# The ending of a top-32 attention with highway layer: the verdict flag through a ones matmul and ScalarE, hints ahead of the skip branch, and spare matmuls

## Chip, cores and metric

One core of a Trainium2 chip runs the whole program. The metric is the device time in microseconds (us) of one launch; the median of several launches is quoted. The five engines are TensorE (PE in the profile, with PEld for its weight loads), VectorE (DVE), ScalarE (ACT), GpSimd (POOL) and SyncE (SP), which mostly issues DMAs. Each has an instruction stream of its own and waits for the others through semaphores.

## What is computed

The inputs are `q`, `k`, `v` of shape 8 x 8 x 576 x 64 (batch, heads, rows, head width) and a highway layer on the 4608 x 512 matrix of all heads side by side.

```python
scores = scale * np.matmul(q, k.transpose(0, 1, 3, 2))
kth = np.partition(scores, -top_k, axis=-1)[..., -top_k:-top_k + 1]   # top_k = 32
scores = np.where(scores >= kth, scores, -1000000000.0)
attn = np.exp(scores - np.max(scores, axis=-1, keepdims=True))
attn = attn / (np.sum(attn, axis=-1, keepdims=True) + 1e-09)
x = heads_side_by_side(np.matmul(attn, v))
H = np.maximum(x @ w_h, 0.0)
T = 1.0 / (1.0 + np.exp(-(x @ w_t + b_t)))
out = (T * H + (1.0 - T) * x).astype(np.float32)
```

## The kernel before, in words

Query rows are taken in groups of 128 of one batch; a group holds eight heads, and two heads (a "pair", `n`) are worked on at a time: 144 pairs in 144 steps (lines 1006 to 1099), about 5.6 us each. In step `n`, PE makes the scores of pair `n+1` (`scores`, line 220), ACT copies them into a buffer `z` (`evac`, line 242), DVE folds and searches the scores of earlier pairs for the 32nd largest value (`tree`, `folds`, `tops`, `rest`, with POOL computing the minima of the folds), ACT makes a penalty `pen` from the threshold (`mask`), PE transposes score plus penalty (`trans`, `parts`), ACT takes the exponential into `et`, and PE multiplies with the values (`av`) five steps after the scores. The highway layer of a finished group (`ffn_x`, `ffn_h`, `ffn_t`, `ffn_d`, `ffn_e`, `ffn_o`) is spread over later steps.

The class `PinnedCore` (line 41) keeps every instruction of the five engines in the order in which the source issues it, except what is issued through plain `nc.sync`. All pinned instructions are therefore shown with line L36; they are told apart by their tiles. Each engine takes its instructions strictly in order, so an instruction that waits holds up all behind it.

After the loop comes a hand-written ending (lines 1101 to 1167) for the last three pairs, `m` = 141 to 143, the group before the last (`gp`) and the last group (`gl`):

- `ffn_x`, `ffn_h`, `ffn_t` of `gp` run on PE; `final_norm(gl, i0, i1)` (line 592) divides a stretch of columns of the last group by its sums: DVE writes `scales` and then `x`.
- `final_turn(gl, i0, i1, bank)` (line 607) lets PE transpose these columns into `xtps`, and DVE (or ACT, for one middle stretch) scale them into `xT`. It is done for the columns 0 to 2, then 2 to 3, then 3 to 4 (in units of 128). `final_h` and `final_t` multiply `xT` with the two weight matrices on PE.
- `ffn_d(gp)`, `ffn_e(gp)`, `ffn_o(gp)` are DVE's last work on `gp` (tiles `xh`, `d`, `d`, `o`; 512 columns each), and SP sends `o` away (line 791).
- `judge_lists`, `judge_scales`, `judge_last` (lines 980 to 993) reduce checks over the whole run to one number per partition, `bad`: whether the fast search of the 32nd value may have been wrong for any row.
- `final_o` (line 655) makes the last group's output in two halves on DVE: `d`, `o`, then SP sends the first half away, then `d`, `o`, then ACT sends the second. Only then `judge` (line 995) turns `bad` into one integer: PE transposes it into a row (`bps`), DVE takes the maximum (`flag_f`) and casts it (`flag`).

Every engine then loads `flag` into a register (line 1169) and branches (line 1170): if it is above 0, a general path (lines 1171 to 1212) computes everything anew, in a loop over batches; otherwise all engines jump over it to the end of the program, where SP waits for every DMA queue and all engines meet. With these inputs the general path is skipped. The general path is long: the jump passes some 1,340 instructions on PE, 520 on DVE, 170 on ACT, 150 on SP and 50 on POOL.

`WARM` (line 23) and `spin` (line 949) already put matmuls of no use into the opening: `spin(n)` multiplies the zero tile `idle` with itself `n` times into a PSUM tile of the pool `ztps`.

Of the kernel before, what the change touches and what calls it, by code (L numbers as in the profile page):

```python
# [9 lines left out]
ALU = mybir.AluOpType  # L10
AX = mybir.AxisListType
FP32 = mybir.dt.float32
# [7 lines left out]
J = 4  # L20
NZ = 3
NPEN = 3
WARM = {1: 9, 2: 7, 3: 8}


# [43 lines left out]
class Ops:  # L69
# [582 lines left out]
            if i1 == n_g:  # L652
                nc.scalar.activation(tp, tp, AF.Tanh)

    def final_o(self, g, dsts, queues, finish):


        vec, P = self.nc.vector, self.P
        W = self.dm // 2
        n = P // len(dsts)  # L660
        o = self.fpool.tile([P, self.dm], FP32, tag="o", name="o")
        for j, tp in enumerate(g.tp):
            cs = slice(j * W, (j + 1) * W)
            vec.scalar_tensor_tensor(
                out=g.d[:, cs], in0=tp, scalar=1.0, in1=g.d[:, cs],
                op0=ALU.add, op1=ALU.mult,
            )
            vec.tensor_tensor(o[:, cs], g.d[:, cs], g.x[:, cs], ALU.subtract)
            for i, dst in enumerate(dsts):
                queues[j].dma_start(dst[:, cs], o[i * n : (i + 1) * n, cs])  # L670
        finish()

    def ffn_bank(self, g, name, other=False):
        if g.last:
# [120 lines left out]
def kernel(  # L795
# [10 lines left out]
    nc = tc.nc  # L806
    P = nc.NUM_PARTITIONS
# [13 lines left out]
    def const(shape, dt, name):  # L821
        return consts.tile(shape, dt, tag=name, name=name)
# [20 lines left out]
    for i in range(2):  # L843
        vt = const([P, H, nck, DE], BF16, f"v{i}")
        nc.gpsimd.memset(vt[:], -1.0)
        vbufs.append(vt)
    cst = const([P, P], BF16, "cst")
    nc.gpsimd.memset(cst[:], 0.5 / float(P))
    room = const([P, NG, H, 4], FP32, "room")
# [15 lines left out]
    with ExitStack() as cm:  # L865
# [18 lines left out]
        def out_rows(g):  # L884
            if not g.rem:
                r0 = g.b * S + g.qt
                return [out[r0 : r0 + JP : J, :]]
            ends = [(g.b + i) * S for i in (0, 1)]
            return [out[r1 - R : r1, :] for r1 in ends]
# [56 lines left out]
        ops.load_first(pr, queue, 2, H)  # L946
        ops.load_rest(pr, "krest", queue, 2, H)
        ops.load(pr, "kin", 2, queue)
        def spin(n):
            if n:  # L950
                warm = ops.ztps.tile([P, 512], FP32, tag="zt", name="warm")
            for _ in range(n):
                ops.nc.tensor.matmul(
                    warm[:], idle[:, 0:P], idle[:], start=True, stop=True
                )
# [17 lines left out]
        step = 0  # L973
        ok = const([P, 4], FP32, "ok")
        bad = const([P, 5], FP32, "bad")
        flag_f = const([1, 1], FP32, "flag_f")
        flag = const([1, 1], I32, "flag")
        vec = ops.nc.vector

# [14 lines left out]

        def judge():
            bps = ops.zrps.tile([P, 512], FP32, tag="zr", name="bps")
            ops.nc.tensor.transpose(bps[0:1, 0:P], bad[:, 4:5], ident[:])
            vec.tensor_reduce(flag_f[:], bps[0:1, 0:P], op=ALU.max, axis=AX.X)
            vec.tensor_copy(flag[:], flag_f[:])

        late, fill, opening = [], [], []
        def values(m):
            g, pi = pairs[m]
            ops.av(m, g, pi, preps[g.b]["vb"])

        while step <= NPR:
            n = step
            if have(n):
                ops.tree(n)
                if n < 2:  # L1010
                    ops.minima(n, ops.folds(n, *pairs[n], []))
                    opening += ops.lists(n, *pairs[n])
                    ops.run(opening, 1)
                elif n % 2:
                    nq = n // 2 + 1
                    ops.minima(nq, ops.folds(nq, *pairs[n - 1], fill))
                    fill = []
                if NHP <= n + 1 < 2 * NHP:
                    ops.turn(pr, "qin", n + 1 - NHP, None, 1)
                if n == NHP:  # L1020
                    ops.load(pr, "qin", 3, None, None, 1)
                if n == 2 * NHP:
                    ops.turn_rest(pr, 0, NHP, ("qrest",))
            if n == 5:
                load_weights()
            if have(n - 4):
                ops.mask(n - 4, *pairs[n - 4], tis=(0,))
            kind = fg = None
            nextg = None
            if ffn and (ffn[0][0] != "x" or n % 2):  # L1030
                kind, fg = ffn.pop(0)
                if kind == "t" and ffn and ffn[0][0] == "x":
                    nextg = ffn.pop(0)[1]
            if have(n - 5):
                values(n - 5)
            if have(n - 4):
                ops.mask(n - 4, *pairs[n - 4], tis=(1,))
            if have(n + 1):
                g, pi = pairs[n + 1]
                ops.scores(n + 1, g, pi, preps[g.b])  # L1040
                ops.evac(n + 1)
                if n + 2 < NHP:
                    ops.turn(pr, "kin", n + 2, True)
            spin(WARM.get(n, 0))
            if kind == "x":
                ops.ffn_x(fg)
            if kind == "h":
                ops.ffn_h(fg)
                ops.ffn_r(fg)
                ops.ffn_d(fg)  # L1050
            if nextg:
                ops.ffn_x(nextg)
            if kind == "t":
                ops.ffn_t(fg)
                if n < NPR - 1:
                    ops.ffn_e(fg)
                    ops.ffn_o(fg, *out_rows(fg))
            if n == 3:
                ops.values_rest(pr)
                ops.values(pr, 0)  # L1060
            if n == 4:
                ops.values(pr, 1)
            ended = False
            if have(n - 5):
                g, pi = pairs[n - 5]
                ended = pi == len(g.pairs) - 1 and (not g.rem or g.r0 > 0)
            if n % 2:
                gens = ops.lists_rest(n // 2 - 1, *pairs[n - 3]) if have(n - 3) else []
                late = gens[2:]
                gens = gens[0:2]  # L1070
                ops.run(gens)
                ops.run(late, 2)
            else:
                ops.run(late)
                if n == 2:
                    gens = opening
                else:
                    gens = ops.lists(n - 2, *pairs[n - 2]) if have(n - 2) else []
                ops.run(gens, 2 * (n > 2))
                if ended:  # L1080
                    ops.norm(pairs[n - 5][0])
                ops.run(gens, 3)
                if have(n + 1):
                    gens, fill = gens[0:2], gens[2:4]
                ops.run(gens)
            if have(n - 4):
                ops.trans(n - 4)
            if ended and not pairs[n - 5][0].last:
                ops.norm_heads(pairs[n - 5][0])
            for piece in pieces.pop(n, []):  # L1090
                piece()
            if n % 2 == 0 and have(n - 3):
                g, pi = pairs[n - 3]
                if pi == len(g.pairs) - 1:
                    ops.settle(g)
            if ended:
                g = pairs[n - 5][0]
                ffn += [("x", g), ("h", g), ("t", g)]
            step += 1
# [12 lines left out]
        ops.ffn_o(groups[-3], *out_rows(groups[-3]))  # L1112
        ops.mask(m, *pairs[m])
        values(m - 1)
        ops.trans(m)
        ops.ffn_x(gp)
        values(m)
        late = ops.lists_rest(m // 2 + 1, *pairs[m + 1])
        gens, late = late[0:2], late[2:]
        ops.run(gens)  # L1120
# [7 lines left out]
        ops.final_norm(gl, 0, 2)  # L1128
        ops.trans(m + 1)
        ops.ffn_r(gp)  # L1130
        ops.ffn_d(gp, h)
        judge_lists()
        judge_scales()
        part, ends = ops.parts(
            m + 2,
            banks[3],
            (banks[0], ops.fps.tile([P, 512], FP32, tag="fp", name="zt")),
        )
        ends()
        part(0)  # L1140
        part(1)
        values(m + 1)
        ops.final_turn(
            gl, 0, 2, ops.ztps.tile([P, 512], FP32, tag="zt", name="xtps")
        )
        ops.ffn_tanh(gp)
        gl.ps = ops.fps.tile([P, 512], FP32, tag="fp", name="hps")
        ops.final_norm(gl, 2, 3)
        ops.ffn_e(gp)
        values(m + 2)  # L1150
        ops.final_h(gl, 0, 2)
        ops.final_turn(
            gl, 2, 3, ops.ztps.tile([P, 512], FP32, tag="zt", name="xtps")
        )
        ops.final_norm(gl, 3, 4)
        ops.ffn_o(gp, *out_rows(gp))
        ops.final_t(gl, 0, 2)
        ops.final_turn(
            gl, 3, 4, ops.ztps.tile([P, 512], FP32, tag="zt", name="xtps")
        )  # L1160
        ops.final_h(gl, 2, 3)
        ops.final_t(gl, 2, 3)
        judge_last(gl)
        ops.final_h(gl, 3, 4)
        ops.ffn_d(gl)
        ops.final_t(gl, 3, 4)
        ops.final_o(gl, out_rows(gl), (nc.sync, ops.nc.scalar), judge)

    taken = nc.values_load(flag[0:1, 0:1], min_val=0, max_val=1)
    with tc.If(taken > 0):  # L1170
        with tc.For_i(0, B, 1) as b:
            with ExitStack() as cm:
                ops = Ops(cm, tc, shared, exact=True)
# [69 lines left out]
```

## Time and profile before

| what | value |
|---|---|
| median of 4 runs | 834.43 us (833.31, 834.35, 834.52, 834.64) |
| profiled execution, its own time | 833.48 us |
| its span, first to last instruction | 831.7 us |
| DVE busy | 814.8 us, 98% of the span |
| ACT, POOL, PE busy | 91%, 85%, 85% |
| mean granted clock of PE | 0.985 |
| chain that ended last, by engine | DVE 91%, PE 3%, ACT 2%, POOL 2%, issue 1% |
| last busy instruction (DVE's cast into `flag`) | 824.67 to 824.81 us |

How to read it: the profiled execution lasted 1.78 us longer than its span, which lies around the first and the last instruction. The profile counts as busy only what an engine itself computes; register loads, branches, semaphore waits and DMA issues are done by an engine's sequencer and have a "q" after the engine's name (DVEq). The chain of waits goes back from the last busy instruction, so what comes after 824.8 us has to be read from the instructions of the lines 1169, 1170 and 1238 (the program's end).

### The profile page before, as it was taken

How to read it: one execution, taken by the hardware profiler on the slowest of the kernel's cores; microseconds unless marked ns; L12 is line 12 of the kernel's file. 1: busy time of each engine (PE TensorE's matmuls, PEld its weight loads, DVE VectorE, ACT ScalarE, POOL GpSimd, SP SyncE). 2: the span in 40 equal slices, each digit the busy share in tenths (PEclk: the TensorE clock that was granted, in tenths of full speed). 3: DMA queues.
4: the chain of work that ended last, by engine and by line, in shares of the span. 5: the costliest groups of instructions: out<-in, count | busy, mean ns of one | idle time of the engine just before them, and what ended most of it. 6: DMA issues, size and time to landing. Idle time of an engine off the chain costs nothing.

```text
span 831.7 us, 20149 instructions
## 1 busy us (share of the span) xinstructions
PE 703.1 (85%) x6586; PEld 486.6 (59%) x6586; DVE 814.8 (98%) x4176; ACT 760.9 (91%) x1522; POOL 708.8 (85%) x457
## 2 busy tenths in 40 slices
PE   8788888888898888788888898878988888888874
PEld 4565566565666555565566565656556665555553
DVE  5999999999999999999999999999999999999996
ACT  4899999899999999899999999989999999988984
POOL 5888888789889888888889988888888989887991
PEclk9999999999999999999999999999999999999998
DMA  7564334234153432333325242323413211111221
GB/s 182 137 107 84 65 90 77 60 71 93 29 109 77 77 90 38 73 65 72 83 52 101 63 113 39 65 58 65 115 39 67 50 27 39 40 39 27 40 39 43
DMA packets 105184, 58.12 MB, mean 70 GB/s; under 512 B 82288, under 2 KB 91888, under 8 KB 105072
## 3 DMA queue, kind: packets, MB, share of 16 engines
q1 hardware_dynamic: 93200, 37.47, 17.3%
q0 software_dynamic: 11056, 19.01, 15.9%
q8 instruction: 53, 0.87, 0.4%
q14 instruction: 59, 0.48, 0.2%
q10 hardware_dynamic: 816, 0.30, 0.1%
HBM read 30.67 MB, written 18.35 MB: 59 GB/s over the span
## 4 chain that ended last, share of the span: by engine, by line
DVE 91%; PE 3%; ACT 2%; POOL 2%; issue 1%; DMA 0%; DVEq 0%; POOLq 0%
DVE w L36 51%; DVE m L36 19%; DVE hi L36 11%; DVE hh L36 6%; DVE h L36 3%; PE ps L36 1%; POOL hh L36 1%; POOL hi L36 1%; ACT z L36 1%; PE warm L36 1%; ACT x L36 0%; DVE scales L36 0%; DMA out_dram<-t 0%; ACT pen L36 0%; POOL t L36 0%
## 5 line engine op out<-in xcount | busy, mean ns | idle before, releaser
L36 PE MATMUL ps<-kq 64*128 64x64 f32 (+3 forms) x1280 | 203.6, 441 | 48.6 <-DVE hi L36 42.2
L36 ACT ACTIVATE pen<-z,m 128x576 bf16<-128x576 f32 x286 | 225.7, 790 | 1.7 <-DVE m L36 1.5
L36 PE MATMUL zt<-ident,z 128*128 128x128 f32 x1140 | 213.2, 280 | 2.3 <-ACT xT L36 2.3
L36 PE MATMUL zt<-nident,pen 128*128 128x128 bf16 x1148 | 205.7, 220 | 0.0
L36 ACT ACTIVATE z<-ps 128x1152 f32<-128x1152 f32 x143 | 161.7, 1131 | 42.7 <-PE ps L36 38.9
L36 POOL TENSOR_TENSOR hi<-z,hi 128x1152 int32<-128x1152 int32 (+1 forms) x72 | 188.2, 2614 | 11.1 <-DVE hh L36 5.5
L36 POOL TENSOR_TENSOR hi<-hi,z 128x1152 int32<-128x1152 int32 (+1 forms) x72 | 189.2, 2628 | 5.6
L36 PEld LDWEIGHTS ps<-kq 64*128 64x128 f32 (+1 forms) x1280 | 103.4, 177 | 143.1 <-issue 80.7
L36 PEld LDWEIGHTS zt<-ident,z 128*128 128x128 f32 x1140 | 161.5, 142 | 17.1 <-ACT xT L36 3.2
L36 ACT ACTIVATE et<-zt 128x512 bf16<-128x512 f32 x287 | 162.0, 601 | 6.0 <-PE zt L36 2.2
L36 POOL TENSOR_TENSOR hh<-hi,hh 128x576 int32<-128x576 int32 x71 | 104.2, 1467 | 71.1 <-DVE w L36 71.0
L36 PEld LDWEIGHTS <-pen 128*128 128x128 bf16 x1440 | 152.3, 106 | 16.2 <-ACT pen L36 10.9
L36 DVE MAX8 m<-w 128x8 f32<-128x168 f32 x576 | 159.0, 315 | 0.0
L36 PE MATMUL zr<-v,et 128*128 128x65 bf16 (+1 forms) x1590 | 98.5, 196 | 48.5 <-ACT et L36 41.4
L36 PEld LDWEIGHTS <-et 128*128 128x128 bf16 (+1 forms) x1600 | 68.8, 101 | 87.6 <-ACT et L36 85.5
L36 DVE MAX8 w<-hi 128x8 f32<-128x288 f32 x288 | 115.7, 441 | 0.0
L36 DVE TENSOR_TENSOR hi<-ps,z 128x576 f32<-128x576 f32 x142 | 104.5, 736 | 0.9 <-ACT z L36 0.9
L36 POOL TENSOR_TENSOR hh<-hh,hi 128x576 int32<-128x576 int32 x71 | 100.3, 1412 | 5.6
L36 DVE MAX8 w<-hh 128x8 f32<-128x72 f32 x576 | 96.7, 218 | 0.0
L36 DVE MATCH_REPLACE8 w<-m,w 128x168 f32<-128x168 f32 x288 | 88.6, 313 | 0.0
L36 PE MATMUL zr<-ident,z 128*128 128x128 f32 x284 | 67.9, 293 | 8.7 <-ACT xs L36 8.7
L36 ACT ACTIVATE x<-xs,scales 128x64 f32<-128x64 f32 x272 | 68.2, 336 | 0.0
(104 smaller groups left out, 1168.8 us busy)
## 6 DMA issues: line engine op xcount, KB each, us to landing
x<-d POOLq DMA_DIRECT2D x34, 256.0 KB, 3.9
vin<-in_v_dram SPq DMA_DIRECT2D x8, 1024.0 KB, 5.4
kin<-in_k_dram SPq DMA_DIRECT2D x63, 128.0 KB, 3.3
out_dram<-d SPq DMA_DIRECT2D x30, 256.0 KB, 2.3
out_dram<-t POOLq DMA_DIRECT2D x30, 256.0 KB, 4.1
qin<-in_q_dram SPq DMA_DIRECT2D x56, 128.0 KB, 2.9
qrest<-in_q_dram SPq DMA_DIRECT2D x8, 128.0 KB, 3.2
vrest<-in_v_dram SPq DMA_DIRECT2D x8, 128.0 KB, 3.1
```

The source lines that it names most:

```text
L36: return self._tc.keep_in_program_order(fn(*args, **kw))
```

## The change

The verdict is moved off DVE and ahead of `final_o`: `bad` is multiplied with a column of ones (a new constant, set by POOL at the start), which gives the sum over partitions in one number, and ACT copies it into the integer `flag`. The two DVE instructions `flag_f` and `flag` go. In program order, ACT makes this copy ahead of its DMA of the second half, and SP loads the flag before it issues the DMA of the first half.

Ahead of `final_h(gl, 3, 4)` every engine gets one hint instruction that says that its branch at line 1170 will be taken, that is, that the general path will be jumped over.

The ending is reordered: `final_turn(gl, 0, 2)` is moved from behind `values(m + 1)` to ahead of `ffn_d(gp)`, with a PSUM tile from `fps` in the place of one from `ztps`; `parts` takes its second tile from `ztps` in exchange; `ffn_e(gp)` and `ffn_o(gp)` are moved from behind the second and third `final_norm` to behind the last `final_turn`.

Spare matmuls: 3 ahead of the scores in step 133 and 8 in step 134 (`NPR - n` is 11 and 10), and 3 and 2 in the ending, into a bank that is free.

```diff
+ENGINES = [
+    getattr(mybir.EngineType, e) for e in ("PE", "DVE", "Activation", "Pool", "SP")
+]
+IDLE = {11: 3, 10: 8}
...
+    ones = const([P, 1], FP32, "ones")
+    nc.gpsimd.memset(ones[:], 1.0)
...
-            ops.nc.tensor.transpose(bps[0:1, 0:P], bad[:, 4:5], ident[:])
-            vec.tensor_reduce(flag_f[:], bps[0:1, 0:P], op=ALU.max, axis=AX.X)
-            vec.tensor_copy(flag[:], flag_f[:])
+            ops.nc.tensor.matmul(
+                bps[0:1, 0:1], bad[:, 4:5], ones[:], start=True, stop=True
+            )
+            ops.nc.scalar.copy(flag[:], bps[0:1, 0:1])
...
                 g, pi = pairs[n + 1]
+                spin(IDLE.get(NPR - n, 0))
                 ops.scores(n + 1, g, pi, preps[g.b])
...
         values(m - 1)
+        spin(3, banks[3])
         ops.trans(m)
         ops.ffn_x(gp)
         values(m)
+        spin(2, banks[3])
...
         ops.ffn_r(gp)
+        ops.final_turn(
+            gl, 0, 2, ops.fps.tile([P, 512], FP32, tag="fp", name="xtps")
+        )
         ops.ffn_d(gp, h)
...
-        part, ends = ops.parts(
-            m + 2,
-            banks[3],
-            (banks[0], ops.fps.tile([P, 512], FP32, tag="fp", name="zt")),
-        )
+        part, ends = ops.parts(m + 2, banks[3], (banks[0], None))
...
         values(m + 1)
-        ops.final_turn(
-            gl, 0, 2, ops.ztps.tile([P, 512], FP32, tag="zt", name="xtps")
-        )
...
         ops.final_norm(gl, 2, 3)
-        ops.ffn_e(gp)
         values(m + 2)
...
         ops.final_norm(gl, 3, 4)
-        ops.ffn_o(gp, *out_rows(gp))
         ops.final_t(gl, 0, 2)
         ops.final_turn(
             gl, 3, 4, ops.ztps.tile([P, 512], FP32, tag="zt", name="xtps")
         )
+        ops.ffn_e(gp)
+        ops.ffn_o(gp, *out_rows(gp))
         ops.final_h(gl, 2, 3)
         ops.final_t(gl, 2, 3)
         judge_last(gl)
+        tc.no_sync_barrier()
+        tc.mark_branch_hint_location("checked", "LikelyTaken", list(ENGINES))
+        tc.no_sync_barrier()
         ops.final_h(gl, 3, 4)
         ops.ffn_d(gl)
         ops.final_t(gl, 3, 4)
-        ops.final_o(gl, out_rows(gl), (nc.sync, ops.nc.scalar), judge)
+        judge()
+        ops.final_o(gl, out_rows(gl), (nc.sync, ops.nc.scalar))
 
-    taken = nc.values_load(flag[0:1, 0:1], min_val=0, max_val=1)
-    with tc.If(taken > 0):
+    taken = nc.values_load(flag[0:1, 0:1], min_val=0, max_val=P)
+    with tc.If(taken > 0, label="checked"):
```

## Prediction

> **What bounds the kernel.** I read the page's busy times first, then the chain of waits, then the timeline from 810 us on, then the instructions of the branch.
>
> ```profile
> PE 703.1 (85%) x6586; PEld 486.6 (59%) x6586; DVE 814.8 (98%) x4176; ACT 760.9 (91%) x1522; POOL 708.8 (85%) x457
> ```
>
> DVE is busy 814.8 of 831.7 us, and the list of its waits shows almost none between 20 us and 815 us. So in the 144 steps only what delays DVE counts. The change puts nothing on DVE there. It reorders DVE's last 10 us, and it changes what follows them: DVE ends at 824.8 us, but the span at 831.7 us. Where these 6.9 us go is seen in the instructions of line 1170, the skip (engine, operation, count, duration in ns, first and last start in us):
>
> ```profile
> L1170 SPq EVENT_SEMAPHORE  x8: 17/17/17, 829.5 to 830.0; - x8
> ...
> L1170 ACTq COMPARE_BRANCH  x1: 62/62/62, 825.4 to 825.4; - x1
> L1170 PEldq COMPARE_BRANCH  x1: 3518/3518/3518, 825.4 to 825.4; - x1
> L1170 DVEq COMPARE_BRANCH  x1: 72/72/72, 825.5 to 825.5; - x1
> L1170 SPq COMPARE_BRANCH  x1: 45/45/45, 825.7 to 825.7; - x1
> ...
> L1170 ACTq EVENT_SEMAPHORE  x1: 17/17/17, 825.9 to 825.9; - x1
> ...
> L1170 DVEq EVENT_SEMAPHORE  x1: 21/21/21, 829.4 to 829.4; - x1
> ```
>
> All engines branch within 0.3 us. ACT goes on 0.4 us later. PE stays 3.5 us in its branch; DVE and SP execute nothing for 3.8 us behind theirs. In this gap the trace has 16 KB and 8 KB packets on the two instruction queues, from 826.5 us on: the jump's target is being fetched. From SP's first semaphore wait (829.5) to the end are 2.2 us, passed by SP's 20 waits and the last meeting of the engines. The output's last DMA (ACT, issued 824.48, 1.9 us to landing) is down at 826.4, long before. **So the end is flag, load (0.5 us), branch, a 3.8 us fetch, 2.2 us of waits.**
>
> **The change, part by part.**
>
> *Flag.* Two DVE instructions go (0.20 and 0.14 us, 0.36 us from 824.45 to 824.81). A 1x1 matmul and a 1x1 copy on ACT come. Neither is in the trace; the nearest rows are the transpose into `bps` (0.27) and ACT's copy of 128x130 (0.26), so 0 to 0.6 us for both. ACT has nothing else to do between its last tanh (822.6) and its DMA issue, and the copy hides behind the two `d` and two `o` of `final_o`. I put it at 0. After it each engine loads the flag behind its own last work: DVE behind `o`, ACT behind its DMA issue. SP now loads before it issues the first half (0.7 us with the two register steps); the half is made by DVE later than that, so the issue is not late.
>
> *Hints.* One instruction per engine. No row shows one; other sequencer instructions take 17 to 72 ns (above), so 0 to 0.1 us, taken as 0. What a hint saves lies between 0 (no effect) and 3.8 us (DVE, SP), 3.5 us (PE). I take the full saving: the nearest row is ACT's own branch in this trace, which goes on after 0.4 us because its target was there. The hints stand 2.5 to 3.3 us ahead of the branches in the sums below, so up to 1.3 us of a fetch may be left; it lies behind the landing of the last DMA.
> The Trainium skill, "Runtime: NRT & Kernel Launch", section "Instruction fetch mechanics", speaks against this edit: prefetch there is purely sequential, and a taken branch out of the loaded window forces a fetch. It names no hint. By it the sum would be that of rival 1. The same section gives TensorE room for 2048 instructions; PE's jump over some 1,340 stalled all the same, so here the row decides.
>
> *Reordered ending.* Here the trace speaks against the change:
>
> ```profile
> 814.61 0.47 DVE L36 TENSOR_TENSOR x<-xs,scales 128x256 f32<-128x256 f32 x1
> 815.01 0.41 DVE L36 TENSOR_SCALAR xh<-x 128x512 f32<-128x512 f32 x1
> ...
> 815.85 0.28 PE L36 MATMUL t<-ident,z 128*128 128x128 f32 x1
> ...
> 817.89 0.41 PE L36 MATMUL xtps<-ident,x 128*128 128x128 f32 x2
> ...
> 820.68 0.30 PE L36 MATMUL xtps<-ident,x 128*128 128x128 f32 x1
> ...
> 821.05 0.28 DVE L36 TENSOR_SCALAR xT<-xtps 128x128 bf16<-128x128 f32 x1
> ...
> 824.02 0.43 DVE L36 TENSOR_TENSOR o<-d,x 128x256 f32<-128x256 f32 x1
> ```
>
> First stall. `xT` of columns 0 to 2 now stands directly behind `x` on DVE and waits for two transposes, which stand on PE behind `trans(m+1)`. PE is through with that at 815.85 (its next work, `t<-ident,z`, starts there). The transposes take 0.41, handing over 0.07 (820.98 to 821.05): `xT` starts at 816.33. DVE could have gone on at 815.01, so it idles 1.32 us; before, it lost 0.22 us here to a DMA that is now down in time. **DVE is 1.1 us late**, and its next `scales` (819.05 before) comes at 820.15.
>
> Second stall. Before, `d` and `o` of `gp` (0.60 us each from start to start) filled DVE while PE transposed the later columns. Now they stand behind the last `xT`. Chain: `scales` 820.15, `x` 820.34, transposes 0.39 later at 820.73, six matmuls of `final_t` between the two transposes (819.63 to 820.68 before, 1.05), so the last transpose at 821.78 and `xT` 0.37 later at 822.15, while DVE has nothing from 821.0 on. Before, it was at 821.05: still 1.1 us late. Behind it come `xT` 0.20, `d` 0.71, `o` 0.60, then the three small ones of `judge_last` (0.55 without the 0.19 us wait for PE they had): the last group's `d` starts at 824.2, before at 821.97. **DVE's end is 2.2 us later**: the last `o` runs from 826.25 to 826.7.
>
> *Spare matmuls.* In the opening one costs 0.216 us (7 more in a row, 1.51 us between starts). Three in step 133 lie in a PE gap of 2.18 us (747.13 to 749.32), three in the ending in one of 1.15 us (before 808.91), two in one of 0.33 us: 0 to 0.1 us late, taken as 0. Eight in step 134 meet no gap before the scores: these shift from 755.17 to 756.90 and end at 758.2 instead of 756.5. ACT takes them at 758.47, busy with `pen` until 758.45; 0.25 us of cover is left, and DVE's `hi<-ps,z` at 759.64 starts just behind ACT's end. Cost 0. Their use is the clock:
>
> ```profile
> 745.90:749.30 3.40, 0.85 (x13) 0.42 (x10) 3.40 (x15) 2.45 (x5) 3.24 (x3) 1.00 0.19 34
> 749.30:752.70 3.40, 3.38 (x15) 2.05 (x16) 3.40 (x28) 0.88 (x1) 3.32 (x2) 0.50 0.00 0
> ```
>
> (stretch, sum, busy PE, PEld, DVE, ACT, POOL, granted clock.) After 3.4 us with PE busy 0.85 us it got half clock for 3.4 us, yet DVE stayed busy throughout (3.40): worth 0 here, up to about 1 us in runs where it falls on a step that DVE waits on. In this run too, 674.2 to 677.6 with 1.90 us busy was followed by half clock.
> "TensorE: Matmul & The Clock Gate", section "Why this matters for your kernels", asks only that PE have no idle gaps over about 3 us; by it none of these matmuls is needed and their worth is 0, which leaves the sum as it is. The row is stricter: gaps of at most 2.2 us sufficed.
>
> **Sum.** ACT issues the last DMA at 826.25 + 0.46 = 826.7, it lands 1.9 us later at 828.6, and SP finds its engines' branches and its own done. The DMA's semaphore is one of the first of SP's waits; the rest and the meeting take 1.9 to 2.2 us, I take 2.0: end 830.6 instead of 831.7, **1.1 us less**. Against the profiled execution (833.48) that is 832.4; it lay 0.95 us under the median, and I subtract from the median: 834.43 - 1.1 = **833.3 us**. A measurement of this kernel can tell about 0.2% (1.7 us) from no change: faster means under 832.8, slower over 836.1.
>
> **Rivals.**
> 1. *The hints do nothing* (they carry the wrong target, or the fetched code is displaced). SP branches after its DMA issue: first half made at 825.9, issued until 826.2, fetch 3.75, so waits from 830.0 and the end at 832.2: +0.5, 834.9 us. For it: no row shows a hint at work.
> 2. *DVE's stalls are smaller than I worked out.* Without any, the last DMA lands at 826.4 as before and the end is at 828.4: 831.1 us; half of them give 832.2. Against it: in-order engines and the rows above; also POOL's 3,993 ns drain behind the branch (826.0 to 830.0), which, if it doesn't shrink, holds the end at about 830.8.
> 3. *The spare matmuls save about 1 us in most runs* that half clock cost there (three of four runs lie 1.0 to 1.3 us over the fastest): 833.3 - 1.0 = 832.3 us. Against it: the profiled run lost nothing at 749 us.
> 4. *Slower: step 134.* If PE has half clock there, eight spares take 3.4 us, the scores (2.40 at half clock, as at 749.32) end at 761.0 and DVE's `hi` starts at 762.1 instead of 759.64: +2.5 - 1.1 = +1.4, 835.8 us. It decides once the scores end after 758.45. For it: 0.25 us of cover; against it: PE is busy from 749.3 to 755.2. With rival 1 on top it is 837.4.
>
> **Numbers.** Forecast 0.41, rival 1 0.13, rival 2 0.25 (all but 0.01 under 832.8), rival 3 0.12, rival 4 0.09 (0.05 over 836.1). Faster 0.36, same 0.59, slower 0.05. The range goes from rival 2 in full to just over rival 1: 831.1 to 835.3.
>
> **What would show it.** Right: PE's branch under 0.2 us, DVE and SP going on within 0.5 us; instruction packets ahead of the branch; DVE idle 1.3 us ahead of the first `xT` and 1.1 us ahead of the last; the last `o` near 826.3; end 2 us behind the last landing. Wrong: a branch of 3.5 us (rival 1), a last `o` before 825.5 (rival 2), POOL's drain ending last, or DVE waiting for ACT's `z` near 760 us (rival 4).

## The result, and the profile after

The changed kernel takes **833.89 us** (median of 35 runs, 832.13 to 835.52) against 834.35 us for the kernel before (55 runs, 833.08 to 836.69): ratio 0.9991, 95% interval [0.9985, 0.9996], or 0.46 us less by the medians. The prediction of 833.3 us said 1.1 us less. The size is near; the experiments show that the reason given for it is wrong.

The profiled execution of the changed kernel took 835.38 us, 1.5 us over its median, with half clock in 794.07 to 800.90 us just ahead of the ending; lengths in the ending are therefore read from the other runs too.

DVE is busy for 815.1 us, where it was 814.8 before. The instructions of the changed kernel's skip, now line 1178 (engine, operation, count, duration in ns, first and last start in us):

```profile
L1178 SPq EVENT_SEMAPHORE  x8: 17/17/17, 831.3 to 831.8; - x8
...
L1178 PEldq COMPARE_BRANCH  x1: 3827/3827/3827, 827.6 to 827.6; - x1
...
L1178 SPq COMPARE_BRANCH  x1: 70/70/70, 828.7 to 828.7; - x1
L1178 DVEq COMPARE_BRANCH  x1: 84/84/84, 829.3 to 829.3; - x1
...
L1178 DVEq EVENT_SEMAPHORE  x1: 21/21/21, 832.3 to 832.3; - x1
```

PE still stands 3.8 us in its branch. SP goes on 2.5 us behind the end of its branch instruction and DVE 2.9 us, instead of 3.8 us for both (such a time is called a gap below). The branches no longer fall together: the early flag lets PE jump 1.5 us before DVE's last `o` ends. The hints and POOL's drain (line 1246, the end of the program):

```profile
L1246 POOLq DRAIN  x3: 40/112/3995, 828.1 to 833.3; - x3
...
L1246 PEldq BRANCH_PREFETCH_HINT  x1: 50/50/50, 823.8 to 823.8; - x1
L1246 DVEq BRANCH_PREFETCH_HINT  x1: 56/56/56, 826.2 to 826.2; - x1
L1246 SPq BRANCH_PREFETCH_HINT  x1: 62/62/62, 826.3 to 826.3; - x1
```

A fetch of code is a packet of 16 KB on queue 8 (PE's) or of 8 KB on queue 14 (the other four engines'). From 823.85 to 828.5 us, behind PE's hint, the DMA view of the changed kernel has only packets of outputs (first the sum, then queue: packets, MB, share):

```profile
DMA packets 144, 0.26 MB, mean 56 GB/s; under 512 B 16, under 2 KB 16, under 8 KB 144
...
q1 hardware_dynamic: 144, 0.26, 15.0%
```

So no code was fetched behind the hints of PE, DVE and SP; PE's packet comes at 828.58, 1.0 us behind its branch. DVE's ending has the stalls that the prediction named (timeline; in brackets idle time before it, and who ended it):

```profile
818.73 0.42 DVE L40 TENSOR_SCALAR xT<-xtps 128x256 bf16<-128x256 f32 x1 [3.10 <-PE xtps L40]
...
824.26 0.29 DVE L40 TENSOR_SCALAR xT<-xtps 128x128 bf16<-128x128 f32 x1 [0.67 <-PE xtps L40]
...
828.63 0.43 DVE L40 TENSOR_TENSOR o<-d,x 128x256 f32<-128x256 f32 x1
```

DVE's last `o` ends 14.33 us behind the start of the first `scales` of the last group (10.08 before), and the span ends 4.47 us behind that `o` (7.27 before). The ending loses in DVE's order what it gains behind DVE. One more reading: from SP's first semaphore wait behind its branch (831.28) to the end are 2.24 us, just as in the kernel before (from 829.48). The last output had landed at 831.48, before SP came to the wait for it, so here the end hangs on SP's return from its branch and not on the landing.

### The profile page after: what moved, and what is told of

Read it like the earlier page. It is cut to its first block, busy times and chain, and to the rows that moved or that the text cites. A ratio compares the mean times of both kernels' runs of the same rounds, so it can differ in the third digit from the quotient of the medians.

```text
span 833.5 us, 20188 instructions
## 1 busy us (share of the span) xinstructions
PE 707.8 (85%) x6603; PEld 488.8 (59%) x6603; DVE 815.1 (98%) x4174; ACT 760.6 (91%) x1523; POOL 709.0 (85%) x458
## 4 chain that ended last, share of the span: by engine, by line
DVE 93%; PE 3%; ACT 2%; POOL 1%; issue 1%; DVEq 0%; POOLq 0%
DVE w L40 52%; DVE m L40 20%; DVE hi L40 11%; DVE hh L40 6%; DVE h L40 3%; PE ps L40 1%; PE zt L40 1%; PE warm L40 1%; DVE scales L40 0%; ACT pen L40 0%; ACT et L40 0%; PE t L40 0%; POOL hh L40 0%; DVE d L40 0%; POOL hi L40 0%
```

## The experiments

My theory after the result: the late hints do nothing; the new order costs DVE some 2 us; the early flag gives it back, because PE, POOL and SP jump beside DVE's last work. Rivals: the hints work in part (the shorter gaps), or the spares' clock is the gain. Each kernel was run beside the kernel before on the same chip; medians, and ratios to it with their 95% intervals, are given.

**1. Without the hints.**

```diff
-        tc.no_sync_barrier()
-        tc.mark_branch_hint_location("checked", "LikelyTaken", list(ENGINES))
-        tc.no_sync_barrier()
```

> The changed kernel without the five branch hints, all else kept. My theory: the hints do nothing, and the changed kernel's shorter gaps behind the branches (DVE 2.9, SP 2.5 us instead of 3.8) come from the branches no longer falling together. Then the gaps stay at 2.5 to 2.9 us, PE's branch at 3.5 to 3.8 us, and the time at that of the changed kernel, 833.9 us, within 0.3. Rival: the hints work in part; then the gaps of DVE and SP go back to 3.8 us and the time rises by about 1 us, to 834.9.

833.58 us, before 834.01: 0.9986 [0.9974, 0.9998]. PE's branch took 3.58 us, SP's gap was 2.5 and DVE's 3.0 us. The shorter gaps are not the hints'.

**2. Without the spares.**

```diff
-                spin(IDLE.get(NPR - n, 0))
...
-        spin(3, banks[3])
...
-        spin(2, banks[3])
```

> The changed kernel without the sixteen spare matmuls, all else kept. My theory: they cost nothing and bring little, so 833.9 us within 0.3. Rival (the gain of the whole change is the spares', through the granted clock): the time rises by about 1 us, to 834.9, and the mean granted clock falls. Other rival (the eight in one step delay DVE): the time falls by up to 1 us.

833.78 us, before 834.01: 0.9994 [0.9985, 1.0003]. In time as the theory had it. But one line contradicted "the hints do nothing" (line 1175 is the skip here):

```profile
L1175 PEldq COMPARE_BRANCH  x1: 487/487/487, 826.3 to 826.3; - x1
```

PE's hint was at 822.52, and from 822.6 to 826.2 us, ahead of the branch, there is a packet of code on its queue (it starts at 823.56):

```profile
q8 instruction: 1, 0.02, 1.7%
```

So a hint can act. The end didn't gain, because it hung on the last landing (at 830.57, with the end 1.99 us behind it) and not on PE.

**3. The old order, with early flag, late hints and spares.**

```diff
+        ops.ffn_e(gp)
         values(m + 2)
...
         ops.final_norm(gl, 3, 4)
+        ops.ffn_o(gp, *out_rows(gp))
         ops.final_t(gl, 0, 2)
...
-        ops.ffn_e(gp)
-        ops.ffn_o(gp, *out_rows(gp))
```

and the first `final_turn` behind `values(m + 1)` again.

> The changed kernel with the order of the ending as before the change; early flag, hints and spares kept. My theory: DVE's two stalls (1.1 us each) go, its last o ends near 824.5 instead of 826.7, and the end comes 2.2 us earlier than in the changed kernel: 831.7 us. Rival: DVE's end isn't what counts behind the early flag (POOL's 4.0 us drain or the fetches hold the end); then the time falls by less than 0.7 us, to 833.2 or more.

831.09 us (5 runs), before 834.01: 0.9965 [0.9951, 0.9979]. First `scales` to last `o`: 10.14 us, as before the change. The new order costs what the theory said.

**4. The early flag alone, on the kernel before.**

```diff
-            ops.nc.tensor.transpose(bps[0:1, 0:P], bad[:, 4:5], ident[:])
-            vec.tensor_reduce(flag_f[:], bps[0:1, 0:P], op=ALU.max, axis=AX.X)
-            vec.tensor_copy(flag[:], flag_f[:])
+            ops.nc.tensor.matmul(
+                bps[0:1, 0:1], bad[:, 4:5], ones[:], start=True, stop=True
+            )
+            ops.nc.scalar.copy(flag[:], bps[0:1, 0:1])
...
-        ops.final_o(gl, out_rows(gl), (nc.sync, ops.nc.scalar), judge)
+        judge()
+        ops.final_o(gl, out_rows(gl), (nc.sync, ops.nc.scalar))
```

> The kernel before with the early flag alone (ones matmul, copy on ACT, ahead of the last sums); no hints, no spares, order as before. My theory: the flag brings it all. PE, POOL and SP branch while DVE still works, so DVE's gap falls from 3.8 to about 2.9 us and its own flag work (0.36 us) goes: the end is 2 to 2.6 us earlier than in the kernel before, 831.7 to 832.3 us. Rival (hints are needed): gaps of 3.8 us stay, 833.6 to 834 us. Rival (spares are needed): about 1 us above the kernel with the old order and spares.

831.87 us, before 834.01: 0.9975 [0.9966, 0.9984], 2.1 us less. The flag alone brings more than the whole change. Behind the last `o` come 4.78 us instead of 7.27. SP's part of the skip (line 1176 here) shows where they went:

```profile
L1176 SPq EVENT_SEMAPHORE  x8: 17/17/17, 826.5 to 827.0; - x8
...
L1176 SPq COMPARE_BRANCH  x1: 45/45/45, 823.5 to 823.5; - x1
```

SP branches 0.38 us ahead of the end of DVE's last `o` (823.89), where before it did so 1.24 us behind it: 1.62 us. Its gap is 2.90 us instead of 3.75: 0.85 us. From its first wait to the end are 2.22 us, as good as before. That is the whole 2.48 us.

**5. The late hints alone, on the kernel before** (the three lines of experiment 1 behind `judge_last(gl)`, and the label on the `If`).

> The kernel before with the five hints alone, flag and order as before. My theory, as corrected by the run without spares (there PE's branch took 0.49 us and a 16 KB packet came 1.0 us behind its hint, ahead of the branch): the hint acts on PE where no new code block was fetched shortly before it, as here, and on no other engine. Then PE's branch takes about 0.5 us, DVE and SP still stop for 3 to 3.8 us, and the time is that of the kernel before less 0 to 0.7 us. Rival (that short branch was chance): PE's branch 3.5 us again, time unchanged. Rival (the hints act on all): gaps under 0.6 us and a time 3 us lower.

834.75 us, before 834.94: 0.9992 [0.9978, 1.0006]. PE's branch took 4.36 us. "Acts on PE where no block was fetched shortly before" is wrong: here PE's last packet was 15 us before the hint. What differs from experiment 2 is that no packet came between the hint (821.71) and the branch (826.5).

**6. The spares alone, on the kernel before** (the three `spin` calls).

> The kernel before with the sixteen spare matmuls alone. My theory: no step gets longer, and the time is that of the kernel before or up to 0.8 us less, where half clock falls away. Rival (rival 4 of the prediction): DVE waits for the delayed scores near 760 us, and the time rises by 1 to 2.5 us. Rival 3 of the prediction: 1 us less, with a higher mean granted clock.

834.82 us, before 834.94: 0.9991 [0.9977, 1.0005]. No effect that can be measured; rivals 3 and 4 of the prediction both fall.

**7. The new order alone, on the kernel before** (the moves of experiment 3 the other way).

> The kernel before with the new order of the ending alone: the first turn moved up, d and o of the group before moved behind the last turn; flag at the end as before, no hints, no spares. My theory: DVE stalls ahead of the first and of the last xT and ends 2.2 to 2.6 us later, and the end follows in full: 836.3 us or more, slower by 0.26 to 0.35%. Rival (the stalls are smaller, or the old ending waited as long elsewhere): under 835.2.

836.95 us, before 834.94: 1.0019 [1.0004, 1.0034], 2.0 us more by the medians; the 0.26 to 0.35% that I expected lie partly inside the interval. The timeline of DVE:

```profile
816.23 0.43 DVE L36 TENSOR_SCALAR xT<-xtps 128x256 bf16<-128x256 f32 x1 [1.19 <-PE xtps L36]
...
821.76 0.29 DVE L36 TENSOR_SCALAR xT<-xtps 128x128 bf16<-128x128 f32 x1 [0.67 <-PE xtps L36]
...
826.02 0.43 DVE L36 TENSOR_TENSOR o<-d,x 128x256 f32<-128x256 f32 x1
```

Both stalls are there. From the first `scales` to the last `o` it took 12.13 us instead of 10.08. By the medians, flag, order, hints and spares, each alone, are worth -2.14, +2.01, -0.19 and -0.12 us: -0.44 together, and the whole change gave -0.46. That the two agree so well is chance: by the ratios the parts add up to -0.23% and the change gave -0.09%, and each part is uncertain by 0.09 to 0.15%.

**8. Old order, early flag, spares, and the hints far ahead.**

```diff
+                if n == 40:
+                    tc.no_sync_barrier()
+                    tc.mark_branch_hint_location("checked", "LikelyTaken", ENGINES[4:5])
+                    tc.no_sync_barrier()
                 spin(IDLE.get(NPR - n, 0))
...
         spin(2, banks[3])
+        tc.no_sync_barrier()
+        tc.mark_branch_hint_location("checked", "LikelyTaken", ENGINES[0:4])
+        tc.no_sync_barrier()
         late = ops.lists_rest(m // 2 + 1, *pairs[m + 1])
```

> The old order of the ending with early flag and spares, as in the run of the old order, but the hints far ahead: on PE, DVE, ACT and POOL some 12 us earlier, ahead of the fetch of the code block that holds the branch, and on SP in the first half of the program. Theory A: a hint acts only if it stands ahead of that fetch; then packets for the jump's target come ahead of the branches, PE's branch is short, and the gaps of DVE and SP fall under 0.6 us. The end then hangs on the last landing and POOL's 4.0 us drain, so the time falls by at most 0.6 us, to 830.5. Theory B: on DVE and SP the hint never acts; gaps stay at 2.5 to 2.9 us and the time at 831.1.

832.24 us, before 834.94: 0.9958 [0.9944, 0.9972]. The skip (line 1186):

```profile
L1186 SPq EVENT_SEMAPHORE  x8: 17/17/17, 825.5 to 828.7; - x8
...
L1186 PEldq COMPARE_BRANCH  x1: 482/482/482, 824.1 to 824.1; - x1
...
L1186 SPq COMPARE_BRANCH  x1: 70/70/70, 824.9 to 824.9; - x1
L1186 DVEq COMPARE_BRANCH  x1: 84/84/84, 825.6 to 825.6; - x1
L1186 DVEq EVENT_SEMAPHORE  x1: 21/21/21, 826.2 to 826.2; - x1
```

All stalls of the jump are gone: PE's branch takes 0.48 us, and the gaps of SP and DVE are 0.5 us. Theory A holds. The hints stood at 809 to 813 us (SP's at 207); the DMA view from 815 to 823.5 us has code packets behind them and ahead of the branches:

```profile
q8 instruction: 1, 0.02, 0.8%
q14 instruction: 2, 0.02, 0.6%
```

Yet against experiment 3 the time gained nothing that can be measured (0.9958 and 0.9965, intervals overlapping). The end now hangs on the output's last landing, as the DMA view from 824.5 to 828.5 us shows (last lines: issues, KB, us to landing):

```profile
q14 instruction: 4, 0.03, 3.4%
q8 instruction: 1, 0.02, 1.5%
issues: line engine op xcount, KB each, median us to landing
out_dram<-o SPq DMA_DIRECT2D x1, 128.0 KB, 3.5
out_dram<-o ACTq DMA_DIRECT2D x1, 128.0 KB, 3.1
```

In the kernel before, from 823.6 to 826.45 us, the same two transfers have no code packet beside them:

```profile
q1 hardware_dynamic: 144, 0.13, 13.6%
q10 hardware_dynamic: 144, 0.13, 13.5%
issues: line engine op xcount, KB each, median us to landing
out_dram<-o SPq DMA_DIRECT2D x1, 128.0 KB, 1.9
out_dram<-o ACTq DMA_DIRECT2D x1, 128.0 KB, 1.9
```

**9. The early hints alone, on the kernel before** (the lines of experiment 8).

> The kernel before with the early hints alone (flag at the end, order and matmuls as before). My rule from the runs so far: a hint redirects its engine's next code packet, and does nothing if none comes between it and the branch. DVE and SP have one, so their gaps fall from 3.8 to 0.5 us. PE has none there in the kernel before, so its branch still takes 3.5 us. The end then hangs on PE's 3.5 us and POOL's 4.0 us drain, which start where they did, so the time falls by 0.2 to 0.6 us only, to 834.0 to 834.5 where the kernel before has 834.7. Rival (PE's hint acts too): PE's branch 0.5 us, end held by POOL's drain alone, the same time. Rival (the end hangs on the last landing, not on the drain): the end 2.0 us behind the landing at 826.4, a time 3 us lower.

833.42 us, before 834.18: 0.9990 [0.9980, 1.0000]. The skip is line 1180, the end of the program line 1248:

```profile
L1180 DVEq COMPARE_BRANCH  x1: 84/84/84, 826.9 to 826.9; - x1
L1180 PEldq COMPARE_BRANCH  x1: 4212/4212/4212, 827.0 to 827.0; - x1
...
L1180 DVEq EVENT_SEMAPHORE  x1: 21/21/21, 827.5 to 827.5; - x1
L1180 PEldq EVENT_SEMAPHORE  x1: 51/51/51, 831.2 to 831.2; - x1
```

```profile
L1248 SPq EVENT_SEMAPHORE  x14: 17/28/2523, 828.2 to 832.2; - x14
...
L1248 POOLq DRAIN  x3: 40/113/3995, 827.4 to 832.0; - x3
```

As the rule had it: DVE and SP short, PE long, since no packet of its own came between hint and branch (807.1, hint 813.4, next 827.7). SP had its other waits behind it at 828.80 us and then stood 2.52 us, until 831.32. It stood for PE: it waited for a semaphore that PE frees with its first instruction behind its branch (831.24 to 831.29). POOL's drain (827.37 to 831.36) ended 0.04 us after SP's wait, so it would have held the end nearly as long. Hints that work on four engines bring little while PE's branch and POOL's drain start where they did.

**10. Experiment 8 with the verdict ahead of the other group's `o`.**

```diff
         ops.final_norm(gl, 3, 4)
+        judge_last(gl)
         ops.ffn_o(gp, *out_rows(gp))
...
+        judge()
         ops.final_h(gl, 2, 3)
         ops.final_t(gl, 2, 3)
-        judge_last(gl)
```

> The kernel with old order, early flag, spares and early hints, with the verdict's three small DVE operations, matmul and copy moved up, ahead of the o of the group before. The flag is there about 1.2 us earlier, DVE's last o about 0.45 us later (0.56 us of work moved, 0.16 us of waiting gone). Theory: there the last output DMA landed 3.05 us after its issue instead of 1.9, because code packets of the engines behind their branches came between its packets; with PE, POOL and SP jumping earlier, it lands after 1.9 to 2.2 us, and the end, 2.0 us behind the landing, comes 0.4 to 0.7 us earlier: 0.996 times the kernel before falls to 0.995. Rival (the late landing comes from something else, or POOL's drain holds the end): the landing stays at 3 us or the end follows the drain; then the time rises by 0.45 us or falls by 1.2 us.

830.68 us (5 runs), before 834.18: 0.9960 [0.9946, 0.9974]. The last landing took 1.99 us instead of 3.05, as the theory of the code packets had it, and DVE's last `o` came 0.44 us later behind the last `scales` (4.84 instead of 4.40). The 0.4 to 0.7 us that I expected aren't seen: 0.9960 against 0.9958 in experiment 8. With 5 runs and intervals of 1.2 us to each side, they aren't ruled out either.

**11. As 10, with both last output DMAs issued by ACT.**

```diff
-        ops.final_o(gl, out_rows(gl), (nc.sync, ops.nc.scalar))
+        ops.final_o(gl, out_rows(gl), (ops.nc.scalar, ops.nc.scalar))
```

> As the run before, and ACT issues both last output DMAs, so that SP jumps without waiting for DVE's first o and its code packet is out of the way too. By the theory of the code packets the last landing comes another 0 to 0.3 us earlier after its issue (1.9 us), and the time is the same or up to 0.3 us lower. Rival: two issues in a row on ACT (0.36 us each) and one queue for both halves make the landing later by 0.3 us or more.

832.12 us, before 834.18: 0.9977 [0.9968, 0.9986]. The rival was right: the second DMA's issue took 0.71 us, and it landed 3.35 us behind its start.

**12. Early flag and early hints alone** (experiment 8 without the `spin` calls of experiment 2).

> The run with the early hints (old order, early flag) without the sixteen spare matmuls: only the early flag and the early hints are left of the change. My theory: without the spares PE has no code packet between its hint and its branch, so PE's branch takes 3.5 to 4.2 us again, while DVE and SP go on after 0.5 us; that holds nothing up, because the end stands 2.0 us behind the last landing, and PE is through before it. So the time is that of the run with spares, 0.996 to 0.9975 of the kernel before (831.2 to 832.2 where that has 834.2). Rival (the spares bring the gain in the runs of the old order): over 832.5. Rival (PE's late branch holds the end): PE's wait is the last that SP finds.

831.79 us, before 834.73: 0.9964 [0.9953, 0.9974]: the spares aren't needed. PE's branch was expected long, but took 1.06 us (at 824.84). A packet of its own had come in between after all, at 823.22. What I had wrong is when PE's packet comes, not the rule.

## Why the prediction was right in size and wrong in reason

**What bounds the kernel.** Right: where the change leaves DVE's 144 steps alone, only the ending counts. But the chain "flag, load, branch, fetch, waits" let the end hang on the last landing once the hints had removed the fetch. The traces show three things that the end can hang on. It hangs on SP's return from its branch in the kernel before, the changed kernel and experiments 4 to 7 (2.22 to 2.24 us ahead of the end; in experiment 1 2.29, with 0.08 spent on DVE). It hangs on the last landing in 2, 3, 8 and 10 to 12 (1.98 to 1.99 us ahead of the end), and on PE's branch in 9. POOL's drain, named in rival 2, took 3,993 or 3,995 ns in every profile and never ended last; in experiment 9 it comes within 0.04 us of it.

**Hints: the failed step.** "I take the full saving" was wrong. The nearest row I chose, ACT's branch that went on after 0.4 us, showed only that a target already there costs nothing; it said nothing about a hint. In the changed kernel the hints saved nothing: PE's branch took 3.83 us, and without the hints (experiment 1) the gaps are the same to 0.2 us. The runs show the rule in its place, on PE, whose code has a queue of its own (us):

| kernel | hint | PE's own packet between hint and branch | branch |
|---|---|---|---|
| changed | 823.83 | none (821.37 before the hint) | 3.83 |
| 3 | 820.34 | none (818.91) | 3.77 |
| 5 | 821.71 | none (806.5) | 4.36 |
| 9 | 813.43 | none (807.1) | 4.21 |
| 2 | 822.52 | 823.56 | 0.49 |
| 8 | 812.37 | 819.46 | 0.48 |
| 10 | 814.68 | 821.30 | 0.49 |
| 11 | 812.63 | 819.13 | 0.49 |
| 12 | 813.67 | 823.22 | 1.06 |

In nine of nine kernels PE's hint acted when PE's next code packet came between hint and branch, and only then. A packet alone doesn't do it: in experiments 1, 6 and 7, which have no hint, one came at 820.02, 820.98 and 825.18 us, and the branches took 3.58, 3.51 and 3.49 us. Nor does time: 13.5 us between hint and branch did nothing in experiment 9, and 3.7 us were enough in experiment 2. That the packet then brings the jump's target is inferred from the short branch; the traces have no addresses. Except in experiment 2 that packet came 6 to 10 us behind the hint, so there it wasn't the hint that set its time. DVE's and SP's gaps fit too (2.5 us or more with the hint at 821 to 826 us, 0.5 with it at 808 to 809 and 207), but four engines share queue 14, so there I can't name the packet.
The Trainium skill, "Runtime: NRT & Kernel Launch", section "Instruction fetch mechanics", says that prefetch is purely sequential. For a hint that comes too late, that is what the changed kernel did; experiment 8 shows an exception, 0.5 us where the same jump cost 2.5 to 4.1.

**Flag: a term put at 0 that is worth 2.1 us.** The instructions cost nothing, as I said. I saw the early loads and looked only for harm in them. What they bring is SP's earlier branch (1.62 us in experiment 4) and its shorter gap (0.85 us). The forecast has neither, since there the hints had removed the wait; rival 1 has the earlier branch, with a gap of 3.75 us. With the 2.54 us that the changed kernel's profile shows, rival 1's 834.9 us become 833.7, against 833.89 measured. So it is rival 1, which I gave 0.13, that happened, and the forecast was near by luck: it took 3.4 us off the time behind the last `o` by hints that did nothing (7.27 to 3.9), where 2.8 came off by the flag (to 4.47; 4.44 in experiment 1, without hints).

**Reordered ending: right.** 2.2 us were predicted, and experiment 7 has 2.05 from the first `scales` to the last `o`. First stall: 1.32 us of idle time predicted, 1.19 measured. Second stall: 1.1 us of idle time predicted, 0.67 measured; but behind the last `scales` DVE took 5.95 us instead of 4.40, of which 0.60 is the `d` of the other group moved in, so 0.95 us were lost there against 1.1. Not seen: the first stall grows when half clock falls shortly before, because DVE now waits there for a PE that is late. With half clock in 794.5 to 797.9 us it was 2.30 us (experiment 1), in the changed kernel's profile, where it lasted until 800.9, 3.10:

```profile
794.07:797.50 3.43, 3.05 (x10) 1.47 (x11) 3.43 (x26) 0.72 (x2) 3.35 (x2) 0.50 0.00 0
797.50:800.90 3.40, 3.40 (x18) 2.34 (x17) 3.40 (x19) 1.84 (x4) 2.92 (x3) 0.50 0.20 77
```

(stretch, sum, busy PE, PEld, DVE, ACT, POOL, granted clock.) DVE is busy throughout, but ACT, fed by PE, falls behind. In experiments 2 and 7, the other two profiles with the new order, there is no half clock between 777 us and the ending, and the stall is 1.19 us in both. That the half clock causes the longer stall is read from these four profiles, not tried.

**Spare matmuls: right in cost, wrong in place.** 0 was predicted; experiments 2 and 6 show no effect that can be measured. I had put the eight into a step without a gap; they ran from 746.92 us, in the gap of 2.2 us that I had counted for the three. What they did change is where the half clock falls. A half clock that begins at 748 to 752 us stands in all seven profiles without them and in none of the seven with them; one that begins at 794 to 796 us stands in five of the seven with them (changed, 1, 6, 10, 11) and in none without. That is close ahead of the ending, where the new order makes DVE wait for PE. Why it comes there isn't shown.

**The last 2 us.** Right in part: where the last landing decides, the end stands 2.0 us behind it. In the changed kernel it doesn't decide: it came at 831.48 us, and SP, back from its branch at 831.28, found it done. The landing itself took 2.4 us, not 1.9. In every profile but that of experiment 11 the packets of ACT's last DMA begin 0.86 us behind its issue. Where no code packet runs between that point and the landing (the kernel before and the other four with the flag at the end), it lands after 1.9 us. With 0.8 to 1.0 us of code packets in that time (durations added up) it took 2.0 to 2.4 us (changed, 1, 10), with 1.0 to 1.2 us 2.6 (3, 4), and with 1.9, 2.2 and 3.0 us 2.8, 3.1 and 3.2 (2, 8, 12). So the early flag sends the code fetches into the output's way. That costs nothing where SP is back later still (changed, 4); it holds the end in 2, 3, 8 and 12. Experiment 10 moved the fetches and the landing followed; the cause is supported by that, not settled.

**Open.** PE's code packets near the end come 244 to 279 recorded PE instructions apart, and with the spares, which add 32, the last one ahead of the branch comes by 821.4 us in all seven profiles. Without them the next packet seems to be due close to the branch: it came ahead of it in experiments 2, 7 and 12 and not in the kernel before, 4, 5 and 9. Which instruction decides isn't explained. Nor is what PE does for 1.3 to 1.4 us between the end of the packet that its branch waits for and its next instruction.

## What to carry to other kernels

Put the verdict of a rarely taken path as early as its inputs allow: engines that have finished then pay load, branch and fetch beside the work of the one that has not (2.1 us here, the best single part). Look first for the engine whose return the end hangs on, here SP. A branch hint belongs far ahead, before the engine's last code packet in front of the branch; look for that packet in the trace between hint and branch. The best kernels here (early flag with the old order) take 0.996 to 0.998 of the time before, 2 to 3.5 us less; that early hints add to this isn't shown. When a stall of 3.8 us goes, count first what stands just behind it, here PE's branch, a drain of 4.0 us and a landing of 1.9.

## What the runs showed of the hardware that was not expected

- A branch hint takes 45 to 62 ns. On PE it made the branch short (0.5 us, 1.06 in one kernel) where a code packet of PE came between hint and branch, and did nothing where none came (table above).
- SP and DVE stood 3.4 to 4.1 us behind their branches when all five engines branched within 0.3 us (before, 5, 6, 7), and 2.5 to 3.0 us when the branches were spread over 2.2 to 2.5 us (changed, 1 to 4). PE's branch doesn't follow that: 3.5 to 4.4 and 3.6 to 3.8 us.
- A long branch of PE is 0.8 to 1.1 us until its packet starts, 1.1 to 2.1 us of packet, and 1.3 to 1.4 us behind it (nine profiles).
- POOL's drain at the end of the program takes 3,993 or 3,995 ns in all 14 profiles.
